# Spectral mixer with a token MLP: the channel transform back, even frequencies as two row-half products

## The chip, the cores and the metric

The kernel runs on one core of one Trainium2 chip. The metric is the device time of one launch in microseconds (us); the numbers below are medians over runs, and one further execution was taken by the hardware profiler.

## The reference

With x of 2048 tokens by 512 channels, everything in float32:

```
xn = layernorm(x, axis=-1)
s  = irfft2(rfft2(xn, axes=(tokens, channels)) * (w_r + 1j * w_i))       # global filter
h  = layernorm(xn, axis=-1)
u  = gelu(einsum("bsd,sf->bdf", h, w1) + b1)          # MLP over the tokens, F = 1792
g  = silu(einsum("bdf,fs->bds", u, w2) + b2) transposed back to tokens x channels
out = x + s * g
```

So there are two halves that meet in a product: a two-dimensional Fourier filter, and an MLP that mixes tokens.

## The kernel before, in words

Tokens lie in 16 tiles of 128. The Fourier transforms are written as matrix products with tables of cosines and sines that the host lays out (`_constants`): one along the channels, one along the tokens, and the same two backwards. The MLP's products are made from float32 numbers split in a high and a low part, three products for one (`hh`, `hl`, `w2f`); its second layer also uses a seven-product scheme in place of eight (`FORMS`, `ORDER`, `form_a` to `form_d`).

The work runs in three stages on TensorE. First the hidden layer of the MLP, with the forward transform over the tokens in its gaps. Then the rest of the hidden layer, with the filter. Last the stage that the change touches: a loop over `p` from 0 to 7, each block making two tiles of output tokens, `p` and `p + 8`.

A block `p` consists, on TensorE, of seven groups of products (`products(p, n)`, `n` in the order 1, 2, 5, 6, 3, 7, 4; each group 21 matmuls of a 128x128 stationary block of w2, tile `w2f`, against 256 moving columns). In one slot between two groups, which `SLOTS` fixes by hand (after the sixth group in most blocks, after the fourth in the last), stand the two small transforms of the spectral half: `spectral(p - 1)`, the token transform of the block before (tiles `y` and `cft`, 64x64 corners of the array), and `channels(p)`, the channel transform back (tiles `yt` and `cd`; the table `ci` is loaded over `cd`).

`channels(p)` before: for each of the two token tiles `i` and each of four groups `b` (real part of even k, real part of odd k, imaginary part of even k, of odd k; k is the channel frequency) one matmul of 128 frequencies by 128 tokens, stationary, against 128 columns of the table. Its result for `i` fills bank 6 + `i` of PSUM. By the mirror symmetry of the cosines the kernel needs only half the channel positions here; `unfolded(p)` makes the others by sums and differences.

`unfolded(p)` before: ScalarE copies the odd half from PSUM to `es`; VectorE adds and subtracts even and odd (two operations of 512 columns a partition, tile `es`); two more VectorE operations of 512 columns, real plus and minus imaginary part, write `y`, which `spectral(p)` reads in the next block's slot (in the last block, one group of products later). The letters of `SLOTS` say after which group each of the three pieces is put in the queues: an `s` is one piece of `unfolded`, a `g` one copy that makes the next `yt`.

Around them, in each block, ScalarE and VectorE split the next w2 tiles (`w2_high`, `w2_low`, tile `w2f`), add up w2 blocks (tile `a`), sum the products (tile `c`), apply the gate (`gate`, tile `g`) and multiply it with the spectral half (`finish`, tile `r`); GpSimd issues the loads of tile `s` and the stores to `out`. In this stage everything goes through `Kept`, which holds each engine to the order of the program, so an operation that is added to VectorE delays all that stand behind it in its queue.

A float32 matmul appears in the profile as two TensorE records (two passes), one of a product with `w2f` as one.

Of the kernel before, what the change touches and what calls it, by code (L numbers as in the profile page):

```python
# [12 lines left out]
AF = mybir.ActivationFunctionType  # L13
# [3 lines left out]
P = 128  # L17
# [27 lines left out]
def _k1(lo, hi):  # L45

    (t, h), s = divmod(hi, 2), 2 * lo + hi // 2
    return (64 - s if s else 32) if h else s


def _pairs(lo, t):


    if 2 * lo + t == 0:
        return np.array([[1, 0, 1, 0], [1, 0, -1, 0], [0, 1, 0, 0], [0, 0, 0, 1]], float)
    return np.array([[1, 0, 1, 0], [0, 1, 0, 1], [1, 0, -1, 0], [0, -1, 0, 1]], float)


def _constants():


    q = np.arange(P)
    a = 2 * np.pi * (np.outer(q, np.arange(32)) % P) / P
    f = np.stack([np.cos(a), np.sin(a)], 2)
    f[0::2, 0, 1], f[1::2, 0, 1] = np.cos(np.pi * q[0::2] / 2), np.sin(np.pi * q[1::2] / 2)
    f = np.concatenate([f[0::2], f[1::2]]).reshape(P, 64)

    a = 2 * np.pi * (np.outer(2 * np.arange(P) + 1, KD) % (2 * D)) / (2 * D)  # L70
    fd = np.stack([np.cos(a), -np.sin(a)])
    fd[1, :, 0] = np.cos(np.pi * np.arange(P))
    fd = fd.reshape(2, P, 2, P).transpose(0, 2, 1, 3).reshape(4, P, P)
    iv = fd.transpose(0, 2, 1) * 2.0 / (D * S)
    iv[0, 0] *= 0.5
    iv[2, 0] *= 0.5

    g = np.zeros((P, 8, 2, 32, 2))
    back = np.zeros((8, 2, P, 2, 64))
    freq = np.zeros((P, 8, 2), int)  # L80
    j = np.arange(16)
    for lo in range(16):
        for hi in range(4):
            k1, (n, l), (t, h) = _k1(lo, hi), divmod(lo, 2), divmod(hi, 2)
            for r in range(16):
                rows = cr, sr = np.arange(16) * 2 + hi * 32, np.arange(16) * 2 + hi * 32 + 1
                out = np.zeros((2, P))
                if k1:
                    k = [k1 + 128 * r] * 2
                    th = 2 * np.pi * ((j * k[0]) % S) / S  # L90
                    out[0, cr], out[0, sr] = np.cos(th), -np.sin(th)
                    out[1, cr], out[1, sr] = -np.sin(th), -np.cos(th)
                elif r == 0:
                    k = [0, S // 2]
                    out[0, cr], out[1, cr] = 1.0, np.cos(np.pi * j)
                else:
                    k = [128 * r if r < 8 else 64 + 128 * (r - 8)] * 2
                    th = 2 * np.pi * ((j * k[0]) % S) / S
                    out[0, rows[r >= 8]], out[1, rows[r >= 8]] = np.cos(th), -np.sin(th)
                rows = slice(64 * t, 64 * t + 64)  # L100

                out[:, rows] = np.einsum("sajb,abhc->shjc", out[:, rows].reshape(2, 2, 16, 2),
                                         _pairs(lo, t).reshape(2, 2, 2, 2)).reshape(2, 64)
                p = [l * 64 + 2 * (h * 16 + r) + c for c in range(2)]
                for s in range(2):
                    g[rows, n, l, h * 16 + r, s] = back[n, t, p[s], 0] = out[s, rows]
                    freq[p[s], n, t] = k[s]
                if k[0] == k[1]:
                    back[n, t, p[0], 1], back[n, t, p[1], 1] = -out[1, rows], out[0, rows]
                else:  # L110
                    back[n, t, p, 1] = out[:, rows]
    freq = freq.reshape(P, 16)


    ft = np.concatenate([np.concatenate([f[:64].T, f[64:].T], 1)] * 2)
    c = {
        "c_f": f.astype(np.float32),
        "c_ft": ft.astype(np.float32),
        "c_d": fd.transpose(1, 0, 2).astype(np.float32),
        "c_i": iv.transpose(1, 0, 2).astype(np.float32),  # L120
        "c_g": g.transpose(1, 0, 2, 3, 4).astype(np.float32),
        "c_h": back.transpose(0, 2, 1, 3, 4).astype(np.float32),
        "c_t": (np.array([-1.0, -2.0]) * np.where(q % 2, -1.0, 1.0)[:, None]).astype(np.float32),
    }
    return c, freq
# [13 lines left out]
def spectral_mixer_kernel(tc, x, w1, b1, w2, b2, wk, we, wx, c_f, c_ft, c_d, c_i, c_g, c_h, c_t, out):  # L139
    nc = tc.nc  # L140
    V, A, G, T, SY = nc.vector, nc.scalar, nc.gpsimd, nc.tensor, nc.sync
# [17 lines left out]
    with tc.tile_pool(name="ps", bufs=1, space=PSUM) as psp, ExitStack() as left, ExitStack() as right:  # L159
        ps = psp.tile([P, 8, 512], F32, name="ps")  # L160
# [8 lines left out]
        e1 = pers.tile([P, 16, 2], F32, name="e1")  # L169
# [78 lines left out]
        def new_h(j):  # L248
            return lnp.tile([P, D], F32, name=f"h{j}", tag="h", bufs=3)
# [186 lines left out]
        T = Kept(T, keep)  # L436
# [22 lines left out]
        h = new_h(0)  # L459
# [20 lines left out]
        for j in range(NJ):  # L480
# [11 lines left out]
            if j in (8, 10, 12, 14):  # L492
                q = slice(16 * (j - 8), 16 * (j - 6))
# [7 lines left out]
            if more:  # L501
                w = w1_tiles(j + 1)
                h = new_h(j + 1)
# [26 lines left out]
            if more:  # L530
                low(w[1][1], raws[j + 1, 1], w[1][0])
                if FIRST <= j < FIRST + NE:
                    i = j - FIRST
# [210 lines left out]
        for n in range(8):  # L744
            a, b, c, d, e, f = PACE[n]
            u, v, w = ([None] * (k < MADE[n]) for k in range(3))
# [89 lines left out]
        ci = cd  # L836
# [57 lines left out]
        V, A, SY, G = (Kept(e, keep) for e in (nc.vector, nc.scalar, nc.sync, nc.gpsimd))  # L894
# [3 lines left out]
        def new_sums(p):  # L898
            return (fp.tile([P, 2, 2, 2, P], F32, name=f"es{p}", tag="es"),
                    fp.tile([P, 2, 2, 2, P], F32, name=f"y{p}", tag="y"))  # L900
# [18 lines left out]

        def channels(p):  # L920

            yt = yts.pop(p)
            for i in range(2):
                pe = ps[:, 6 + i].rearrange("p (h b c) -> p h b c", b=2, c=P)
                for b in range(4):
                    T.matmul(pe[:, b % 2, b // 2], yt[:, i, b].rearrange("p e c -> p (e c)"), ci[:, b],
                             start=True, stop=True)

        def unfolded(p):

            pe = ps[:, 6:8].rearrange("p i (h k) -> p i h k", h=2)
            es, y = new_sums(p) if p else first_sums
            e0, e1 = (es[:, :, k].rearrange("p i b c -> p i (b c)") for k in range(2))
            A.activation(e1, pe[:, :, 1], AF.Copy)
            V.tensor_add(e0, pe[:, :, 0], e1)
            V.tensor_sub(e1, pe[:, :, 0], e1)
            yield
            u, v = es[:, :, :, 0], es[:, :, :, 1]
            V.tensor_add(y[:, :, :, 0], u, v)
            yield  # L940
            V.tensor_sub(y[:, :, ::-1, 1], u, v)
            ys[p] = y.rearrange("p i h q c -> p i (h q c)")
            yield

# [31 lines left out]
        for p in range(NP):  # L976
# [8 lines left out]
            for k, n in enumerate(ORDER):  # L985
# [23 lines left out]
                if k == slot:  # L1009
                    if p:  # L1010
                        spectral(p - 1)
                    channels(p)
                    pieces = unfolded(p)
                    if p:
                        for g, j in zip(gates.pop(p - 1), (j0 - 1, j1 - 1)):
                            finish(g, j, whole)
# [51 lines left out]
```

## Time and profile before

| | us |
|---|---|
| median of 3 runs (lowest, highest) | 377.51 (377.26, 377.56) |
| the profiled execution, its own time | 377.27 |
| its span, first to last instruction | 375.5 |
| TensorE busy in matmuls | 365.3 (97%) |
| VectorE busy | 300.2 (80%) |
| ScalarE busy | 211.9 (56%) |
| GpSimd busy | 86.7 (23%) |
| mean granted TensorE clock | 0.993 |

Times in rows of the profile are from the start of the span. PE is the matmul side of TensorE and PEld its weight loads, which overlap; DVE is VectorE, ACT is ScalarE. A row of the timeline gives start, length, engine, line, operation, destination and sources, shapes, how many instructions were merged, and in brackets how long the engine had been idle and what ended that. Line 136 is that of the helper class that records every operation, so groups are told apart by their tiles.

### The profile page before, as it was taken

How to read it: one execution, taken by the hardware profiler on the slowest of the kernel's cores; microseconds unless marked ns; L12 is line 12 of the kernel's file. 1: busy time of each engine (PE TensorE's matmuls, PEld its weight loads, DVE VectorE, ACT ScalarE, POOL GpSimd, SP SyncE). 2: the span in 40 equal slices, each digit the busy share in tenths (PEclk: the TensorE clock that was granted, in tenths of full speed). 3: DMA queues.
4: the chain of work that ended last, by engine and by line, in shares of the span. 5: the costliest groups of instructions: out<-in, count | busy, mean ns of one | idle time of the engine just before them, and what ended most of it. 6: DMA issues, size and time to landing. Idle time of an engine off the chain costs nothing.

```text
span 375.5 us, 8397 instructions
## 1 busy us (share of the span) xinstructions
PE 365.3 (97%) x3274; PEld 314.1 (84%) x3274; DVE 300.2 (80%) x564; ACT 211.9 (56%) x381; POOL 86.7 (23%) x128
## 2 busy tenths in 40 slices
PE   7999999999999999999999999999999999999991
PEld 4778888777887777877888999898989999898981
DVE  5799999965799987999985978676959685867771
ACT  4787888748534437545347675465464556464520
POOL 3133333331222202221020010230404040504031
PEclk9999999999999999999999999999999999999997
DMA  6967997407695596985493687798869787886343
GB/s 199 276 159 182 234 304 236 168 0 190 196 241 187 186 250 204 242 241 181 132 289 66 178 231 158 200 168 229 136 220 141 214 158 194 186 195 134 66 56 56
DMA packets 33288, 68.36 MB, mean 182 GB/s; under 512 B 4737, under 2 KB 19505, under 8 KB 33121
## 3 DMA queue, kind: packets, MB, share of 16 engines
q1 hardware_dynamic: 24192, 42.04, 39.5%
q0 software_dynamic: 8656, 25.27, 31.8%
q8 instruction: 25, 0.41, 0.5%
q10 hardware_dynamic: 400, 0.52, 0.5%
q14 instruction: 15, 0.11, 0.1%
HBM read 59.43 MB, written 8.13 MB: 180 GB/s over the span
## 4 chain that ended last, share of the span: by engine, by line
PE 96%; DVE 1%; DMA 1%; ACT 0%; issue 0%; DVEq 0%
PE ps L136 96%; DMA x<-in_x_dram 1%; DVE stm L216 0%; DVE rows L136 0%; ACT g L136 0%; DVE w1l L444 0%; DVE h L246 0%; ACT sdm L222 0%; DVE mvm L226 0%; DVE r0m L230 0%; DVE tm L232 0%; DVE rsm L233 0%; DVE tm L231 0%; DVE v2m L220 0%; DVE v2m L221 0%
## 5 line engine op out<-in xcount | busy, mean ns | idle before, releaser
L136 PE MATMUL ps<-h,w1h 128*128 128x512 f32 x400 | 116.5, 398 | 1.1 <-DVE nbm L235 1.1
L136 PEld LDWEIGHTS ps<-h,w1h 128*128 128x128 f32 x400 | 72.7, 188 | 20.9 <-issue 6.1
L136 PE MATMUL ps<-h,w1l 128*128 128x512 f32 x200 | 68.1, 392 | 0.1
L136 DVE TENSOR_TENSOR w2f<-a,w2f 128x896 fp32r<-128x896 f32 x36 | 39.3, 1092 | 27.8 <-ACT w2f L136 27.8
L136 PEld LDWEIGHTS ps<-h,w1l 128*128 128x128 f32 x200 | 37.2, 188 | 9.4 <-DVE w1l L444 1.6
L136 ACT ACTIVATE w2f<-a 128x896 fp32r<-128x896 f32 x36 | 36.6, 1018 | 13.5 <-issue 7.4
L136 PE MATMUL ps<-fb,w2f 128*128 128x256 f32 x336 | 42.9, 281 | 0.0
L136 PE MATMUL ps<-fa,w2f 128*128 128x256 f32 x336 | 42.3, 280 | 0.0
L136 PEld LDWEIGHTS ps<-fb,w2f 128*128 128x128 f32 x336 | 40.7, 188 | 0.9 <-issue 0.8
L136 POOL DMA_DIRECT2D s<-in_w_dram x14 | 18.2, 1300 | 99.4 <-DMA s<-in_w_dram 61.5
L136 PE MATMUL ps<-fc,w2f 128*128 128x256 f32 x336 | 40.9, 279 | 0.0
L136 PEld LDWEIGHTS ps<-fa,w2f 128*128 128x128 f32 x336 | 40.7, 188 | 0.0
L136 PEld LDWEIGHTS ps<-fc,w2f 128*128 128x128 f32 x336 | 40.1, 188 | 0.0
L136 POOL DMA_DIRECT2D out_dram<-r x28 | 23.7, 1288 | 31.7 <-DVE r L136 31.7
L152 ACT ACTIVATE w1h<-w1s 128x512 fp32r<-128x512 f32 x26 | 16.2, 631 | 20.9 <-PE ps L136 10.3
L626 POOL DMA_DIRECT2D xc<-xc x16 | 9.8, 617 | 70.4 <-ACT xc L624 55.1
L282 POOL TENSOR_TENSOR ey<-t 128x256 f32<-128x256 f32 x16 | 15.7, 981 | 43.5 <-DVE t L280 41.8
L136 DVE TENSOR_TENSOR w2f<-s,w2f 128x896 fp32r<-128x896 f32 x15 | 16.3, 1088 | 8.8 <-ACT w2f L136 8.8
L136 ACT ACTIVATE w2f<-s 128x896 fp32r<-128x896 f32 x15 | 15.4, 1024 | 12.4 <-PE ps L136 11.5
L444 DVE TENSOR_TENSOR w1l<-w1r,w1h 128x384 fp32r<-128x384 f32 x32 | 21.3, 667 | 0.5 <-ACT w1h L441 0.5
L136 PE MATMUL ps<-fd,w2f 128*128 128x256 f32 x168 | 21.1, 279 | 0.0
L136 ACT ACTIVATE g<-c,b2t 128x256 f32<-128x256 f32 x24 | 12.2, 507 | 14.8 <-DVE c L136 14.7
(115 smaller groups left out, 602.3 us busy)
## 6 DMA issues: line engine op xcount, KB each, us to landing
a<-in_w_dram SPq DMA_DIRECT2D x22, 448.0 KB, 3.7
wt<-in_wk_dram POOLq DMA_DIRECT2D x16, 512.0 KB, 5.9
s<-in_w_dram SPq DMA_DIRECT2D x16, 448.0 KB, 4.1
s<-in_w_dram POOLq DMA_DIRECT2D x16, 448.0 KB, 6.3
w1s<-in_w_dram SPq DMA_DIRECT2D x52, 128.0 KB, 5.5
w1r<-in_w_dram SPq DMA_DIRECT2D x28, 192.0 KB, 5.3
xc<-xc POOLq DMA_DIRECT2D x16, 256.0 KB, 3.0
out_dram<-in_x_dram SPq DMA_DIRECT2D x4, 960.0 KB, 7.2
```

The lines of the kernel that those rows point to most:

```text
L136: return lambda *args, **kw: self.keep(operation(*args, **kw))
L152: return A.activation(hi, src, AF.Copy), V.tensor_sub(lo, src, hi.bitcast(F32))
L282: G.tensor_add(ey[:, 0::3, :, j], a, b)
L444: keep(V.tensor_sub(dst, src, hi.bitcast(F32)))
L626: keep(G.dma_start(*(v.rearrange("p s t c -> p s (t c)") for v in (there[c::2], here[1 - c::2, ::-1]))))
```

## The change

For even k, the table's columns at the channel positions q and 127 - q differ only in the sign that k/2 decides: it is one for k divisible by 4 (rows 0 to 63 of `yt`) and the other for the rest (rows 64 to 127). So the change makes two products for each even group, one from each half of the rows, each with 64 columns instead of 128, and writes them to banks 6 and 7; their sum and their difference are the 128 columns that stood there before. The odd groups stay matmuls of 128 rows and 128 columns. In a block there are then 8 matmuls of 64 rows, 128 tokens, 64 columns, and 4 of 128 rows, 128 tokens, 128 columns, in place of 8 of the latter.

ScalarE copies one of the two even halves (256 columns, and one column more) instead of 512 odd columns, into `y`, which serves as room. VectorE makes the even columns with two operations of 256 columns, and then goes on as before, with the odd columns read from PSUM. The order in which the channel positions stand changes with it, and so the table (last lines of the first piece) and the ways in which `y` is written.

```diff
     iv = fd.transpose(0, 2, 1) * 2.0 / (D * S)
     iv[0, 0] *= 0.5
     iv[2, 0] *= 0.5
+    iv[1, :, 64:] *= -1
+    iv[1::2] = np.roll(iv[1::2], 64, 2)
...
         def channels(p):
             yt = yts.pop(p)
             for i in range(2):
-                pe = ps[:, 6 + i].rearrange("p (h b c) -> p h b c", b=2, c=P)
-                for b in range(4):
-                    T.matmul(pe[:, b % 2, b // 2], yt[:, i, b].rearrange("p e c -> p (e c)"), ci[:, b],
+                for s in range(2):
+                    for r, rows in enumerate((slice(0, 64), slice(64, P))):
+                        at = 128 * i + 64 * s
+                        T.matmul(ps[:, 6 + r, at:at + 64], yt[rows, i, 2 * s].rearrange("p e c -> p (e c)"), ci[rows, 2 * s, :64],
+                                 start=True, stop=True)
+            for i in range(2):
+                for s in (1, 0):
+                    at = 256 + 128 * s
+                    T.matmul(ps[:, 6 + i, at:at + P], yt[:, i, 2 * s + 1].rearrange("p e c -> p (e c)"), ci[:, 2 * s + 1],
                              start=True, stop=True)

         def unfolded(p):
-            pe = ps[:, 6:8].rearrange("p i (h k) -> p i h k", h=2)
             es, y = new_sums(p) if p else first_sums
+            other = y.rearrange("p i h q c -> p (i h q c)")[:, :257]
+            low_k, odd = ps[:, 6, :256].rearrange("p (i s c) -> p i s c", s=2, c=64), ps[:, 6:8, 256:]
+            A.activation(other, ps[:, 7, :257], AF.Copy)
+            other = other[:, :256].rearrange("p (i s c) -> p i s c", s=2, c=64)
+
+            V.tensor_add(es[:, :, 1, :, 64:], low_k, other)
+            V.tensor_sub(es[:, :, 1, :, 63::-1], low_k, other)
             e0, e1 = (es[:, :, k].rearrange("p i b c -> p i (b c)") for k in range(2))
-            A.activation(e1, pe[:, :, 1], AF.Copy)
-            V.tensor_add(e0, pe[:, :, 0], e1)
-            V.tensor_sub(e1, pe[:, :, 0], e1)
+            V.tensor_add(e0, e1, odd)
+            V.tensor_sub(e1, e1, odd)
             yield
             u, v = es[:, :, :, 0], es[:, :, :, 1]
-            V.tensor_add(y[:, :, :, 0], u, v)
+            to = y.rearrange("p i h q (n c) -> p i h (q n) c", n=2)[:, :, :, ::-3]
+            V.tensor_add(to, *(t.rearrange("p i h (n c) -> p i h n c", n=2) for t in (u, v)))
             yield
-            V.tensor_sub(y[:, :, ::-1, 1], u, v)
+            V.tensor_sub(y.rearrange("p i h q c -> p i h (q c)")[:, :, ::-1, 64:192], u, v)
```

TensorE, block 3: the slot between the sixth and the seventh group of products. Before (`128x64` and the like are the shapes of the result):

```order
L136 MATMUL ps_58<-fb6_2709,w2f7_3_3470 128x256
L136 MATMUL ps_58<-y2_3350,cft_63 64x512 x4
L136 MATMUL ps_58<-cd_64,yt3_3444 128x128 x8
L136 MATMUL ps_58<-fb2_1480,w2f4_3_3501 128x256
L136 MATMUL ps_58<-fb0_1592,w2f4_3_3501 128x256
```

The same place with the change:

```order
L138 MATMUL ps_58<-fb6_2709,w2f7_3_3488 128x256
L138 MATMUL ps_58<-y2_3366,cft_63 64x512 x4
L138 MATMUL ps_58<-cd_64,yt3_3462 128x64 x8
L138 MATMUL ps_58<-cd_64,yt3_3462 128x128 x4
L138 MATMUL ps_58<-fb2_1480,w2f4_3_3519 128x256
```

Eight whole products became eight of half the rows and half the columns and four whole ones; what stands ahead and behind is the same.

VectorE, from the end of block 2 into block 3: `r` is the gated product of the block before, `es` and `y` are `unfolded`, `a` the sums of w2 blocks, `w2f` the low parts that the coming products read. Before:

```order
L136 TENSOR_TENSOR r_3344<-ps,g_2918 128x2x128 x2
L136 TENSOR_TENSOR es_3349<-ps,es_3349 128x2x256 x2
L136 TENSOR_TENSOR a_3_3179<-a_3_3179,s_11_3146 128x896
L136 TENSOR_TENSOR a_3_3206<-a_3_3206,a_3_3179 128x896
L136 TENSOR_TENSOR w2f_3_3377<-s_11_3146,w2f_3_3377 128x896
L136 TENSOR_TENSOR y_3350<-es_3349 128x4x128
L136 TENSOR_TENSOR w2f_3_3410<-a_3_3179,w2f_3_3410 128x896
L136 TENSOR_TENSOR y_3350<-es_3349 128x2x2x128
L136 TENSOR_TENSOR w2f_3_3437<-a_3_3206,w2f_3_3437 128x896
```

With the change:

```order
L138 TENSOR_TENSOR r_3360<-ps,g_2924 128x2x128 x2
L138 TENSOR_TENSOR es_3365<-ps,y_3366 128x2x2x64 x2
L138 TENSOR_TENSOR es_3365<-es_3365,ps 128x2x256 x2
L138 TENSOR_TENSOR a_3_3191<-a_3_3191,s_11_3158 128x896
L138 TENSOR_TENSOR a_3_3218<-a_3_3218,a_3_3191 128x896
L138 TENSOR_TENSOR w2f_3_3395<-s_11_3158,w2f_3_3395 128x896
L138 TENSOR_TENSOR y_3366<-es_3365 128x4x2x64
L138 TENSOR_TENSOR w2f_3_3428<-a_3_3191,w2f_3_3428 128x896
L138 TENSOR_TENSOR y_3366<-es_3365 128x2x2x128
L138 TENSOR_TENSOR w2f_3_3455<-a_3_3218,w2f_3_3455 128x896
```

Two operations of 256 columns a partition are new, ahead of the two sums of w2 blocks and the low parts; the rest stands in the same order.

## The prediction

> **What bounds the kernel now.** I read the page first: the span, the engines and the chain of work that ended last.
>
> ```profile
> span 375.5 us, 8397 instructions
> PE 365.3 (97%) x3274; PEld 314.1 (84%) x3274; DVE 300.2 (80%) x564; ACT 211.9 (56%) x381; POOL 86.7 (23%) x128
> ...
> PE 96%; DVE 1%; DMA 1%; ACT 0%; issue 0%; DVEq 0%
> ```
>
> TensorE is the chain: 96% of it lies there. Whatever the change takes from TensorE or gives to it in the last stage moves the end, and VectorE counts only where it makes TensorE wait. The view by stretches, over one block of the last stage, shows how much room VectorE has:
>
> ```profile
> core 0: us, PE busy (x) PEld busy (x) DVE busy (x) ACT busy (x) POOL busy (x), PEclk, DMA share, GB/s
> 262.00:282.35 20.35, 20.35 (x174) 19.41 (x173) 15.00 (x23) 10.80 (x17) 5.17 (x6) 1.00 0.76 176
> ```
>
> A block lasts 20.35 us, TensorE is busy for all of it at the full granted clock (1.00), VectorE for 15.00. So 5.35 us a block are free on VectorE, if they lie in the right places. Next I read TensorE's weight loads around one slot, since it is there that eight matmuls change form:
>
> ```profile
> 279.11 0.31 PEld L136 LDWEIGHTS ps<-fb,w2f 128*128 128x128 f32 x2
> 279.55 0.21 PEld L136 LDWEIGHTS ps<-y,cft 64*64 64x64 f32 x8
> 280.57 1.86 PEld L136 LDWEIGHTS ps<-cd,yt 128*128 128x128 f32 x16 [0.81 <-issue]
> 282.35 0.30 PEld L136 LDWEIGHTS ps<-fb,w2f 128*128 128x128 f32 x2
> ```
>
> The eight matmuls of the channel transform are 16 records, and from their first load to the next group's first load is 282.35 - 280.57 = 1.78 us: 0.111 us a record. Half of them are the even groups: 8 x 0.111 = 0.89 us a block, 7.1 us in all eight blocks. That is everything the change has to work with on TensorE.
>
> **What a record costs: the moving columns or the load.** The change halves the moving columns of the even groups, so it matters whether the 0.111 us are set by those columns or by the load of 128x128 weights. The warm-up at the kernel's start has a case that tells these apart, matmuls of single-pass type with 128 moving columns; the products with `w2f` are of the same type with 256:
>
> ```profile
> 5.41 0.72 PE L136 MATMUL ps<-wz 128*128 128x128 f32 x5
> ...
> L136 PE MATMUL ps<-wz 128*128 128x128 f32 x6 | 0.8, 266 | 0.0
> ...
> 262.04 2.54 PEld L136 LDWEIGHTS ps<-fb,w2f 128*128 128x128 f32 x21
> 264.51 2.54 PEld L136 LDWEIGHTS ps<-fd,w2f 128*128 128x128 f32 x21
> ```
>
> 21 products of 256 columns take 264.51 - 262.04 = 2.47 us, 0.118 each. The warm-up's five of 128 columns take 0.72 us with one record's 0.27 at the end, so (0.72 - 0.27) / 4 = 0.112 each. Half the moving columns saved 0.006, not 0.059. At 128 columns of one pass the load sets the pace: 0.112 us for a stationary block of 128x128. The new even records have 64 columns in two passes, as much moving work as those warm-up records, so they too should go at the pace of their loads. What is left is the load of 64 rows by 128 columns, which this trace does not have. The nearest rows are the 64x64 tiles of the forward transform:
>
> ```profile
> L136 PEld LDWEIGHTS ps<-cf,h 64*64 64x64 f32 x512 | 8.3, 134 | 3.2 <-ACT h L242 0.7 <-ACT cf L254 0.7 <-ACT w1h L441 0.7
> ...
> 51.94 1.02 PEld L136 LDWEIGHTS ps<-cf,h 64*64 64x64 f32 x64 [0.35 <-ACT w1h L441]
> 53.03 0.19 PEld L136 LDWEIGHTS ps<-h,w1h 128*128 128x128 f32 x1
> ```
>
> 64 loads on four corners are 16 rounds, and (1.02 - 0.13) / 15 = 0.059 us a round. So tiles that share no rows do load side by side, and a load of half the rows and half the columns takes about half of 0.112. Whether that is for the rows or for the columns the trace can't say. I take the columns: four corners fill the whole array in 0.059 where one whole load takes 0.112, so filling is not limited by the number of cells, while each row has to take twice as many weights one after the other in a block of 128 columns. Then one round of the new pairs, two loads of 64 rows side by side, takes 0.112 as a whole load did, and 16 records in 8 rounds take the same 0.89 us as the 8 whole ones. The even half gains nothing.
>
> The Trainium skill ("TensorE: Matmul & The Clock Gate", section "LDWEIGHTS (loading the stationary operand)") says the same of the load: its time goes by the columns, and few rows take as long as 128. By that rule the even half stays at 0.89 us; no run here shows the shape yet.
>
> **What the change adds on TensorE: two ways of tiling the array where there was one.** Going between 64x64 and 128x128 costs something in the rows above. From the second `fb` load (279.11 + 0.12 = 279.23) to the first of `y` is 0.32 us instead of 0.118: 0.20 more. On the way back, the last round of `cf` begins at 51.94 + 15 x 0.059 = 52.83 and the next whole load at 53.03: 0.20 instead of 0.059, 0.14 more. So the array empties before it goes on in another form, for 0.14 to 0.20 us. Before, a slot has two such changes, `fb` to `y` and `y` to `yt`, and none between `yt` and `fb`. After, the order is `fb`, `y` (64x64), even pairs (64x128), odd groups (128x128): one more in each of the 8 slots, and in block 0, which has no `y`, also one on the way in. I take 0.15 for the way out, nearest to the row with short moving operands, and 0.20 for the way in: 8 x 0.15 + 0.20 = 1.4 us slower. With 0.14 everywhere it is 1.3; with 0.20 everywhere 1.8. If a first matmul after each change waits for its load on top of that, the upper bound rises: the longest of the whole records is 377 ns against 275.
>
> ```profile
> L136 PE MATMUL ps<-cd,yt x128: 270/275/377, 219.6 to 358.7; 128*128 128x128 f32 x128
> ```
>
> That is 0.10 more for nine changes, 1.8 + 0.9 = 2.7 us.
>
> **What it adds on VectorE, and what hides it.** The rows of `es` and `y`, and those of 256 columns:
>
> ```profile
> L136 DVE TENSOR_TENSOR es<-ps,es x16: 678/687/692, 223.5 to 360.3; 128x512 f32<-128x512 f32 x16
> L136 DVE TENSOR_TENSOR y<-es x16: 682/684/687, 228.0 to 362.4; 128x512 f32<-128x512 f32 x16
> ...
> L136 ACT ACTIVATE es<-ps x8: 579/601/602, 222.8 to 359.0; 128x512 f32<-128x512 f32 x8
> ...
> L136 ACT ACTIVATE p<-ps 128x256 f32<-128x256 f32 x12 | 4.6, 385 | 10.5 <-PE ps L136 10.5
> ...
> L136 DVE TENSOR_TENSOR r<-ps,g 128x256 f32<-128x256 f32 x24 | 8.5, 415 | 0.0
> ```
>
> Four operations of 0.68 remain; two of 256 columns come to them, 0.42 each alone. ScalarE's copy falls from 0.60 to about 0.39. So VectorE has 2 x 0.42 = 0.84 us more a block, or 0.66 where operations overlap (four of `r` take 1.41 in the rows below: 0.33 each). Behind them stand the two sums into `a` and the low parts in `w2f`, which TensorE needs. This is the queue after the slot of block 2:
>
> ```profile
> 261.89 1.41 DVE L136 TENSOR_TENSOR r<-ps,g 128x256 f32<-128x256 f32 x4
> 263.21 1.41 DVE L136 TENSOR_TENSOR es<-ps,es 128x512 f32<-128x512 f32 x2
> ...
> 266.66 1.08 DVE L136 TENSOR_TENSOR w2f<-s,w2f 128x896 fp32r<-128x896 f32 x1
> 267.67 0.68 DVE L136 TENSOR_TENSOR y<-es 128x512 f32<-128x512 f32 x1
> 268.63 1.09 DVE L136 TENSOR_TENSOR w2f<-a,w2f 128x896 fp32r<-128x896 f32 x1 [0.28 <-ACT w2f L136]
> 269.64 0.69 DVE L136 TENSOR_TENSOR y<-es 128x512 f32<-128x512 f32 x1
> 270.87 1.09 DVE L136 TENSOR_TENSOR w2f<-a,w2f 128x896 fp32r<-128x896 f32 x1 [0.55 <-ACT w2f L136]
> ...
> 269.57 5.11 PE L136 MATMUL ps<-fc,w2f 128*128 128x256 f32 x42
> ```
>
> The tightest is the `w2f` that ends at 267.74: TensorE starts on that block at 269.57 and reads the low part for the last 7 of its 21 matmuls, from 269.57 + 14 x 0.118 = 271.2. Even 0.84 us late it is there 2.6 us ahead. The gaps of 0.28 and 0.55 then take up the 0.84, and VectorE is on its old times after 270.9. In the last block the result is wanted sooner, one group of products after the slot:
>
> ```profile
> 358.31 1.41 DVE L136 TENSOR_TENSOR r<-ps,g 128x256 f32<-128x256 f32 x4
> 359.63 1.41 DVE L136 TENSOR_TENSOR es<-ps,es 128x512 f32<-128x512 f32 x2
> 361.44 0.42 DVE L136 TENSOR_TENSOR c<-ps,v 128x256 f32<-128x256 f32 x1 [0.41 <-PE ps L136]
> 361.79 1.28 DVE L136 TENSOR_TENSOR y<-es 128x512 f32<-128x512 f32 x2
> ...
> 363.81 1.09 PE L136 MATMUL ps<-y,cft 64*64 64x512 f32 x8
> ```
>
> `y` is ready at 363.07, TensorE takes it at 363.81 when its own turn comes: 0.74 to spare. The wait of 0.41 swallows part of the 0.84, so `y` comes at most 0.43 late, and 0.3 is left. I cost VectorE and ScalarE at nothing; without this cover the last block would cost up to 0.4 us and a whole block's lateness would cost 0.84.
>
> **The sum.** +1.4 us on TensorE, nothing elsewhere. The profiled execution took 377.27 in all with its span of 375.5; its median of three runs is 377.51, 0.24 above. I add to the median: 377.51 + 1.4 = 378.9 us (a span of about 376.9).
>
> **The rivals.** What a measurement of this kernel can tell from no change is about 0.2%, 0.75 us.
>
> *The half-height load takes half the time* (faster). If a load goes by the cells it fills, a round of pairs takes 0.059 like the corners' rounds and the even half of a block falls by 8 x (0.111 - 0.059) = 0.42 us, 3.3 in eight blocks; less the 1.4 that is -1.9, so 375.6. It decides from a round of about 0.09: there the saving, 64 x 0.02, meets the 1.4. For it speaks that the corners' time fits both readings; against it, what each row has to take in. The Trainium skill ("TensorEngine Tiling (Array Packing)", section "Theoretical Speedup") grants up to twice the speed for a dimension of 64 or less, which is this outcome; the rows here show such side by side work only for corners that are small both ways. 0.13.
>
> *No emptying between `y` and the pairs* (the same). Both use halves of the rows; if the array passes from one to the other without the 0.15 to 0.20 that such a change costs, seven slots get 1.05 to 1.4 back and the sum is 0 to +0.35: 377.5 to 377.9, middle 377.7. For it speaks that the row halves are the same in both; against it, that the columns are not. "TensorEngine Tiling (Array Packing)", section "Key Properties", in the Trainium skill, has any change of the mode empty TensorE, so by it this doesn't happen; the rows above agree for the changes they show. 0.13.
>
> *The halves take turns* (the pairs don't run as pairs). Then 16 loads of 0.111 stand where 8 did: +7.1, with the 1.4 it is +8.5, 386.0. Against it speak the corners, where row halves do load side by side. 0.05.
>
> *VectorE reaches the chain*: the new operations write reversed and split columns, and if they took twice as long, 0.84 more a block, the last block's `y` would be 0.5 us late and the tightest `w2f` still in time: +1.9, 379.4. 0.05.
>
> The forecast itself: 0.64. So faster 0.13; the same 0.13; slower 0.64 + 0.05 + 0.05 = 0.74. The range leaves out the faster case and the turns, 0.18: from 377.3, just under the second rival's 377.5 by the spread of the runs, to 377.51 + 2.7 = 380.2.
>
> **What would show it.** In the profile after, the loads of the 64-row matmuls should come in pairs every 0.112 us, 0.9 us for 16, and between the last of them and the first whole load should be about 0.20 - 0.06 + 0.11 = 0.25 us. The slot of blocks 1 to 7, from the first `yt` load to the next `w2f` load, should be 1.9 to 2.0 us instead of 1.78. VectorE's four `es` operations should take about 2.1 us, with no wait of TensorE for VectorE in a block. Loads in pairs every 0.06 us, or a slot under 1.6 us, would make me wrong on the load; a slot at 1.78 wrong on the emptying.

## The result, and the profile after

The changed kernel took 378.88 us (median of 21 runs, 378.39 to 379.70), the kernel before 377.22 (21 runs, 373.29 to 378.41). The ratio is 1.0081, with a 95% interval of 1.0055 to 1.0108: slower by 3.05 us, where 1.4 was forecast. That is the difference of the means, 378.88 against 375.83; the medians are only 1.66 apart, because the median of before happens to fall among its longer times. The time itself, 378.9, is the forecast one; what differs is the kernel before. Its 21 times lie at two levels: ten from 373.29 to 374.32 (mean 373.8) and eleven from 377.22 to 378.41 (mean 377.7). The three runs and the profile that the prediction started from were all of the upper level. The 21 times of the changed kernel lie at one level.

The profile of before was taken at the upper level too. Against it, the profile after differs by what the prediction added. First the page, then TensorE's weight loads around the slot of block 3:

```profile
span 376.9 us, 8549 instructions
PE 366.8 (97%) x3338; PEld 314.9 (84%) x3338; DVE 305.6 (81%) x580; ACT 210.3 (56%) x381; POOL 86.7 (23%) x128
```

```profile
280.27 0.21 PEld L138 LDWEIGHTS ps<-y,cft 64*64 64x64 f32 x8
281.29 2.01 PEld L138 LDWEIGHTS ps<-cd,yt 64*128 64x128 f32 x24 [0.81 <-issue]
283.22 0.30 PEld L138 LDWEIGHTS ps<-fb,w2f 128*128 128x128 f32 x2
```

The span is 376.9, as forecast: 1.4 longer. The slot from the first `yt` load to the next `w2f` load is 283.22 - 281.29 = 1.93 us, against 1.78. From the first load of `y` to the first of `yt` it is 1.02 us, as it was before (280.57 - 279.55). VectorE's queue after the slot of block 2, and its part in the last block with TensorE's next use of `y`:

```profile
262.47 1.41 DVE L138 TENSOR_TENSOR r<-ps,g 128x256 f32<-128x256 f32 x4
263.80 0.75 DVE L138 TENSOR_TENSOR es<-ps,y 128x256 f32<-128x256 f32 x2
264.65 1.41 DVE L138 TENSOR_TENSOR es<-es,ps 128x512 f32<-128x512 f32 x2
265.98 1.08 DVE L138 TENSOR_TENSOR a<-a,s 128x896 f32<-128x896 f32 x1
...
268.10 1.08 DVE L138 TENSOR_TENSOR w2f<-s,w2f 128x896 fp32r<-128x896 f32 x1
...
271.62 1.09 DVE L138 TENSOR_TENSOR w2f<-a,w2f 128x896 fp32r<-128x896 f32 x1 [0.23 <-ACT w2f L138]
...
363.46 1.28 DVE L138 TENSOR_TENSOR y<-es 128x512 f32<-128x512 f32 x2
```

```profile
365.26 1.09 PE L138 MATMUL ps<-y,cft 64*64 64x512 f32 x8
```

From the first `es` to the sum `a` it is 265.98 - 263.80 = 2.18 us instead of 264.54 - 263.21 = 1.33 (the sum `a` of before began at 264.54): 0.85 more. By 271.62 VectorE waits for ScalarE again, so the lateness is taken up, and in the last block `y` is ready at 364.74, 0.52 ahead of TensorE. Nothing here explains the other 1.65 us of the measured 3.05.

### The profile page after: what moved, and what is told of

Same layout as the page of the kernel before. It is cut to its first block, busy times and chain, and to the rows that moved or that the text cites. A ratio compares the mean times of both kernels' runs of the same rounds, so it can differ in the third digit from the quotient of the medians.

```text
span 376.9 us, 8549 instructions
## 1 busy us (share of the span) xinstructions
PE 366.8 (97%) x3338; PEld 314.9 (84%) x3338; DVE 305.6 (81%) x580; ACT 210.3 (56%) x381; POOL 86.7 (23%) x128
## 4 chain that ended last, share of the span: by engine, by line
PE 96%; DVE 1%; DMA 1%; ACT 0%; issue 0%; DVEq 0%
PE ps L138 96%; DMA x<-in_x_dram 1%; DVE stm L218 0%; DVE rows L138 0%; ACT g L138 0%; DVE w1l L446 0%; DVE h L248 0%; ACT sdm L224 0%; DVE mvm L228 0%; DVE r0m L232 0%; DVE tm L233 0%; DVE rsm L235 0%; DVE tm L234 0%; DVE v2m L222 0%; DVE v2m L223 0%
## 5 line engine op out<-in xcount | busy, mean ns | idle before, releaser
L138 PEld LDWEIGHTS ps<-cd,yt 64*128 64x128 f32 (+1 forms) x192 | 15.5, 188 | 6.4 <-issue 4.9
```

The costliest lines, as they stand in the source:

```text
L138: return lambda *args, **kw: self.keep(operation(*args, **kw))
```

## The experiments

**The kernel before, once more; VectorE's part alone; TensorE's part alone; half the columns.** The four ran on one chip and share the runs of the kernel before.

`e1_before` has no edit.

> The kernel before, unchanged. Its 21 times lie at two levels, ten at 373.3 to 374.3 us and eleven at 377.2 to 378.4 us, while the changed kernel's 21 all lie at 378.4 to 379.7. If the two levels belong to the kernel or to the chip and not to the change, this copy shows both levels again, about 3.9 us apart, and its profile falls on one of them: the row-by-row difference to the profile of before then says what the lower level does faster. If the lower level was an accident of that chip, all times lie within 0.5 us of 377.5.

Measured: seven of 12 times from 373.37 to 374.50, five from 377.50 to 378.04, and of the 29 runs of before beside it 22 from 373.37 to 374.80 and seven from 377.23 to 377.88. Both levels are there, and the profile (span 371.6) fell on the lower. The loads of the same products in it, after the slot of block 2:

```profile
259.60 1.86 PEld L136 LDWEIGHTS ps<-cd,yt 128*128 128x128 f32 x16 [0.81 <-issue]
261.38 2.46 PEld L136 LDWEIGHTS ps<-fb,w2f 128*128 128x128 f32 x21
263.77 2.45 PEld L136 LDWEIGHTS ps<-fd,w2f 128*128 128x128 f32 x21
266.15 2.45 PEld L136 LDWEIGHTS ps<-fa,w2f 128*128 128x128 f32 x21
```

The slot is as before (261.38 - 259.60 = 1.78). But 21 products of `fd` take 266.15 - 263.77 = 2.38 us, 0.113 each, where the prediction's rows had 2.47, 0.118. In this execution all products of the last stage up to the slot of block 1 run at 118 ns and all from there on at 113. Those are 43 groups of 21, each 0.09 us shorter: 3.9 us, the distance of the levels. From here on, 113 ns is called the fast rhythm and 118 the slow one.

Neither the clock nor more memory traffic goes with the slow rhythm. Here is one stretch by engines, first in the profile of before, then in this one:

```profile
core 0: us, PE busy (x) PEld busy (x) DVE busy (x) ACT busy (x) POOL busy (x), PEclk, DMA share, GB/s
262.10:278.00 15.90, 15.90 (x137) 15.90 (x137) 11.94 (x18) 8.73 (x14) 4.31 (x5) 1.00 0.76 160
...
262.10:278.00 15.90, 15.90 (x143) 15.90 (x142) 12.31 (x17) 8.59 (x14) 4.32 (x5) 1.00 0.83 177
```

The granted clock is 1.00 in both, and the faster execution moved more by DMA (177 GB/s against 160), not less.

`e2_vector_part`:

```diff
             A.activation(e1, pe[:, :, 1], AF.Copy)
+            V.tensor_add(room_, ps[:, 6, :256], had)
+            V.tensor_sub(room_[:, ::-1], ps[:, 6, :256], had)
             V.tensor_add(e0, pe[:, :, 0], e1)
```

> The kernel before with VectorE's part alone: two more operations of 256 columns ahead of the sums and differences of each block, into room that is overwritten later. TensorE is as before. My theory: hidden, the profiled span stays within 0.2 us of 375.5 and the slot of block 3 (first yt load to the next w2f load) at 1.78 us. Rival, that VectorE reaches the chain: 0.3 to 0.8 us more a block or in the last block, a span of 375.9 to 381. If the extra two operations are what keeps a kernel off the lower level, all times lie near 377.5 and none near 373.7.

Measured: ratio 0.9998 (0.9966 to 1.0029); ten of 12 times from 373.91 to 374.44, two at 377.39 and 377.86. The two operations cost nothing and don't keep the kernel off the lower level. My figure for the span was written for the upper level; the profile fell on the lower, with a span of 372.3 and the slot at 1.78 us as expected. In it the fast rhythm began at the slot of block 2, one block later than in `e1_before`, so the place of the turn is not fixed.

`e3_tensor_part`: `channels` of the change with `unfolded` of before.

> TensorE's part alone: the 64-row pairs and four whole matmuls of the change, but ScalarE and VectorE with the operations of before (a copy of 512 columns, four operations of 512). Left out: the sum and the difference of the halves, and the changed table. My theory: span 375.5 + 1.4 = 376.9, slot 1.92 us, pairs every 0.112 us. If TensorE's part keeps the kernel off the lower level, all times lie near 378.9; if VectorE's part does, some lie near 373.7 + 1.4 = 375.1.

Measured: 378.97 us, six times from 378.86 to 379.22, ratio 1.0109 (1.0067 to 1.0151). No time at the lower level, the products at 118 ns in all blocks. The whole of the result is in TensorE's part. The span, 377.4, is 0.5 over my figure, the time is not; the 0.5 lies ahead of the last stage, where the first `yt` load comes at 220.41 instead of the changed kernel's 219.91.

`e4_half_columns`:

```diff
                 for b in range(4):
-                    T.matmul(pe[:, b % 2, b // 2], yt[:, i, b].rearrange("p e c -> p (e c)"), ci[:, b],
+                    n = P if b % 2 else 64
+                    T.matmul(pe[:, b % 2, b // 2, :n], yt[:, i, b].rearrange("p e c -> p (e c)"), ci[:, b, :n],
```

> The kernel before with 64 instead of 128 moving columns in the even groups, with whole loads of 128x128 and no other form of tiling. Left out: half of the even columns. If the load sets the pace (my theory) the slot stays at 1.78 us and the span at 375.5 although a quarter of the moving work is gone; if the moving columns do, the slot falls by 8 x 0.055 = 0.44 us to 1.34 and the span by 3.5 us to 372.0.

```profile
279.34 1.86 PEld L136 LDWEIGHTS ps<-cd,yt 128*128 128x128 f32 x16 [0.81 <-issue]
281.12 0.19 PEld L136 LDWEIGHTS ps<-fb,w2f 128*128 128x128 f32 x1
```

Measured: slot 281.12 - 279.34 = 1.78 us, no change, though half of the even groups' moving columns are gone; ratio 1.0000 (0.9963 to 1.0036), nine of 12 times at the lower level (373.46 to 374.94). The load sets the pace.

**What in TensorE's part keeps the products at 118 ns.** `e5_corners` cuts the even pairs once more; `e6_more_whole` issues the odd groups twice; `e7_odd_only` is the kernel before without its even groups; `e8_odd_first` has the odd groups ahead of the pairs.

```diff
-                        T.matmul(ps[:, 6 + r, at:at + 64], yt[rows, i, 2 * s].rearrange("p e c -> p (e c)"), ci[rows, 2 * s, :64],
+                        for e in range(2):
+                            T.matmul(ps[64 * e:64 * e + 64, 6 + r, at:at + 64], yt[rows, i, 2 * s, e], ci[rows, 2 * s, :64],
                                  start=True, stop=True)
```

> The changed kernel with the even pairs cut once more, by tokens, into 64x64 corners: 16 matmuls of 64 rows, 64 tokens, 64 columns, in the same form of tiling as y ahead of them. The result is the same. My theory of the load: a round of four corners takes 0.059 us, the even half falls from 0.89 to 0.47 us a block, and the extra change of form is gone in blocks 1 to 7, so -0.42 x 7 - 0.1 = -3.0 us against before at the same rhythm of the products: a span of 372.5 if the products run at 118 ns, 368.6 if most run at 113 ns. On the two rhythms: if the 64x128 form keeps the products at 118 ns, this one shows 113 ns in some executions, as the kernel before does; if eight whole matmuls ahead of the products (instead of 16) keep them there, it never does and all its times lie within 1 us of each other near 374.3.

```profile
278.86 0.21 PEld L138 LDWEIGHTS ps<-y,cft 64*64 64x64 f32 x8
279.34 0.15 PEld L138 LDWEIGHTS ps<-cd,yt 64*64 64x64 f32 x4 [0.28 <-issue]
...
281.23 0.19 PEld L138 LDWEIGHTS ps<-fb,w2f 128*128 128x128 f32 x1
```

```profile
242.11 2.46 PEld L138 LDWEIGHTS ps<-fb,w2f 128*128 128x128 f32 x21
...
256.39 2.46 PEld L138 LDWEIGHTS ps<-fb,w2f 128*128 128x128 f32 x21
...
261.35 2.54 PEld L138 LDWEIGHTS ps<-fb,w2f 128*128 128x128 f32 x21
...
276.18 2.54 PEld L138 LDWEIGHTS ps<-fb,w2f 128*128 128x128 f32 x21
...
281.23 2.46 PEld L138 LDWEIGHTS ps<-fb,w2f 128*128 128x128 f32 x21
```

Measured: 373.14 us, 11 times from 372.74 to 373.68, ratio 0.9917 (0.9886 to 0.9949): faster than the kernel before by the means, though its times overlap with before's lower level (373.42 to 374.68 beside it), and faster than the changed kernel. From the first `y` load to the next product is 281.23 - 278.86 = 2.37 us, 0.43 less than before's 2.80. What I had expected of the rhythm was wrong either way: it is neither kept nor absent, but in this profile changes at every slot from block 1 on (2.46 us for 21 loads is 113 ns, 2.54 is 118).

> The changed kernel with its four odd matmuls issued twice, so that 16 whole records instead of 8 stand between the 64x128 pairs and the products, as many as in the kernel before. At 118 ns a product: 378.9 + 8 x 8 x 0.112 = 386.0 us. If the number of whole records decides the rhythm, some executions fall to the lower level, about 3.9 us below; if the 64x128 form does, none.

Measured: 386.16 us, six times from 385.88 to 386.94; 118 ns throughout. Sixteen whole records don't bring 113 ns back.

> The kernel before with the even groups left out: 8 whole records instead of 16 stand between the 64x64 matmuls and the products, and no other form of tiling. At 118 ns a product: 377.5 - 8 x 0.89 = 370.4 us. If the number of whole records decides the rhythm, all times lie there; if the 64x128 form does, some lie 3.9 us lower, near 366.5.

Measured: three times from 366.87 to 367.59 and three from 370.97 to 371.61. Both levels, with eight whole records. So their number is not what decides.

> The changed kernel with the odd groups ahead of the even pairs, so that the products follow the 64x128 form directly. One more change of form in blocks 1 to 7 than in the changed kernel (64x64 to whole to 64x128 to whole): if a change costs 0.14 to 0.20 us, the span is 1.0 to 1.4 us longer, 377.9 to 378.3, at 118 ns a product. If the change of form costs nothing and the pairs' own pace made the difference, it stays at 376.9. If no whole record ahead of the products lets them start at 113 ns, the lower level shows, near 374.3.

```profile
280.46 0.21 PEld L138 LDWEIGHTS ps<-y,cft 64*64 64x64 f32 x8
281.48 2.06 PEld L138 LDWEIGHTS ps<-cd,yt 128*128 128x128 f32 x24 [0.81 <-issue]
283.60 0.19 PEld L138 LDWEIGHTS ps<-fb,w2f 128*128 128x128 f32 x1
```

Measured: 380.54 us (379.83 to 380.81), all blocks at 118 ns. From the first `y` load to the product is 3.14 us, 0.19 over the changed kernel's 2.95: one more change of form, at the upper end of its price.

**Where the 113 ns are lost.** `e9_half_pairs` has before's matmuls for `p < 4` and the pairs for the rest.

> TensorE as before in blocks 0 to 3 and with the change's pairs in blocks 4 to 7; ScalarE and VectorE as before. Left out: the sum and the difference of the halves, and the changed table. All blocks at 118 ns: 377.5 + 4 x 0.145 = 378.1 us. If a slot with the pairs puts the products back to 118 ns, executions that come to 113 ns in blocks 1 to 3 lose it in block 4 and their times lie between 375.9 and 377.5, none lower. If a slot with the pairs only never lets them in, those executions keep 113 ns and lie near 374.5.

```profile
295.92 2.45 PEld L136 LDWEIGHTS ps<-fb,w2f 128*128 128x128 f32 x21
298.50 0.21 PEld L136 LDWEIGHTS ps<-y,cft 64*64 64x64 f32 x8
299.52 2.01 PEld L136 LDWEIGHTS ps<-cd,yt 64*128 64x128 f32 x24 [0.81 <-issue]
301.45 2.54 PEld L136 LDWEIGHTS ps<-fb,w2f 128*128 128x128 f32 x21
303.92 2.54 PEld L136 LDWEIGHTS ps<-fd,w2f 128*128 128x128 f32 x21
```

Measured: 376.58 us, 11 of 12 times from 375.95 to 377.24 and one at 378.27; the runs of before beside it lie at 373.05 to 374.43 (24) and 377.21 to 377.65 (five). The rows show the moment: the last products ahead of the first slot with pairs run at 113 ns, those behind it at 118, and stay there to the end. Here the pairs do not merely fail to let the fast rhythm in; the slot with them ends it.

`e10_corners_first` puts the corners ahead of `y`; `e11_flip_once` does so from block 2 on; `e12_pairs_first` puts the pairs ahead of `y`:

```diff
                 if k == slot:
+                    evens(p)
                     if p:
                         spectral(p - 1)
-                    channels(p)
+                    odds(p)
```

> The 64x64 corners once more, with the even corners ahead of y instead of behind it, so that the whole odd matmuls follow y directly, as the whole matmuls do in the kernel before. The result is the same. At 118 ns in all blocks 377.5 - 3.0 = 374.5 us. If what decides the rhythm is what stands between y and the products, the two levels of before come back, and the lower is 3.0 us under its 374, near 371. If it is the form of the even half wherever it stands, the products change their rhythm in every block as with the corners behind y, and all times lie near 373.

Measured: 371.92 us, seven of 12 times from 370.77 to 372.02 and five from 374.54 to 375.49; ratio 0.9962 (0.9923 to 1.0000). Two levels (means 371.5 and 375.1), each about 2.3 us below its like of the runs of before beside it (373.8 and 377.4), where 3.0 was expected. The profile fell on the upper, at 118 ns throughout.

> The corners behind y in block 1, where they turned 118 ns into 113 in the profile of the corners, and ahead of y in blocks 2 to 7, where I expect the rhythm to be kept. If the rhythm is set by the slot in this way, all times lie at the lower level, 370.7 to 371.5 us, with none at 374. If the rhythm is chance at each return, times spread from 371 to 374.5.

Measured: three times from 370.92 to 371.61 and nine from 374.50 to 375.56. The profile (375.18 us) stayed at 118 ns behind the slot of block 1, so that slot doesn't turn the rhythm reliably; this expectation fell.

> The changed kernel with one reordering: its 64x128 pairs stand ahead of y instead of behind it, so that the whole odd matmuls and the products follow the 64x64 form of y, as in the kernel before. The result is the same, and so is the number of changes of form. If what stands between y and the products keeps them at 118 ns, both levels come back: 378.9 us at 118 ns and about 375 at 113. If the pairs anywhere in the slot do it, all times stay at 378.4 to 379.7.

Measured: 378.92 us, ten times from 378.52 to 379.40. No lower level: with the pairs at either place the kernel stays at the upper. But not every such slot comes out slow: in its profile the products behind the last slot run at 113 ns (2.46 us). Its rows, first the pairs by themselves in block 3, then that last slot:

```profile
280.31 0.97 PEld L138 LDWEIGHTS ps<-cd,yt 64*128 64x128 f32 x16
281.35 0.21 PEld L138 LDWEIGHTS ps<-y,cft 64*64 64x64 f32 x8
...
357.20 1.06 PEld L138 LDWEIGHTS ps<-cd,yt 64*128 64x128 f32 x16
358.33 0.21 PEld L138 LDWEIGHTS ps<-y,cft 64*64 64x64 f32 x8
359.35 0.97 PEld L138 LDWEIGHTS ps<-cd,yt 128*128 128x128 f32 x8 [0.81 <-issue]
360.24 2.46 PEld L138 LDWEIGHTS ps<-fa,w2f 128*128 128x128 f32 x21
```

Eight rounds of two loads in 0.97 us, (0.97 - 0.19) / 7 = 0.111 a round. In the last slot they took 1.06, so the break was 0.09 us longer there; whether that let the fast rhythm in is not shown.

**The form, or the number of changes.** `e13_corner_between` adds four 64x64 matmuls between before's even and odd groups; `e14_apart` moves the changed kernel's `y` one group ahead, `e15_y_apart` the kernel before's:

```diff
-                if k == slot:
-                    if p:
-                        spectral(p - 1)
+                if k == slot - 1 and p:
+                    spectral(p - 1)
+                if k == slot:
                     channels(p)
```

> The kernel before with one round of 64x64 corner matmuls (four, 64 columns) between its even and its odd whole groups, into columns of PSUM that the odd groups overwrite. The result is the same. That is two more changes of form in every slot and no 64x128 form: 377.5 + 8 x (0.06 + 0.20 + 0.15) = 380.8 us at 118 ns. If the number of changes of form in a slot keeps the products at 118 ns, all times lie there; if the 64x128 form does, both levels show, the lower near 376.9.

Measured: 381.35 us, six times from 381.02 to 381.87; 118 ns in all blocks. So it is not the 64x128 form alone.

> The changed kernel with y taken out of the slot, one group of products earlier: the slot then has two changes of form (products to 64x128 to whole), as many as the kernel before, and y's place two of its own. The result is the same. One more change in blocks 1 to 7: 378.9 + 7 x 0.15 to 0.20 = 380.0 to 380.3 us at 118 ns. If the number of changes in a slot keeps the products at 118 ns, both levels show, the lower near 376; if the 64x128 form does, all times lie near 380.

```profile
258.21 2.45 PEld L138 LDWEIGHTS ps<-fb,w2f 128*128 128x128 f32 x21 [0.81 <-issue]
260.79 2.01 PEld L138 LDWEIGHTS ps<-cd,yt 64*128 64x128 f32 x24
262.71 2.54 PEld L138 LDWEIGHTS ps<-fb,w2f 128*128 128x128 f32 x21
```

Measured: 380.68 us, six times from 380.11 to 380.94. No lower level, with two changes of form in the slot; so it is not three changes in the slot alone either. But the rhythm did turn: in blocks 2, 4 and 6 the one group between `y` and the slot ran at 113 ns, and each time the slot with the pairs put the products back to 118, as the rows show for block 2.

> The kernel before with y taken out of the slot, one group of products earlier. The result is the same. The block still has two changes of form (products to y and back), but the products follow the 64x64 form directly, and the whole matmuls of the channel transform follow products without a change. At 118 ns 377.5 us, as before. If the number of changes of form in a block decides (two let the products at 113 ns, three or four don't), both levels show, the lower near 374. If the products must come from whole float32 matmuls that follow a change of form, as in every kernel so far that reached 113 ns, all times lie near 377.5.

```profile
257.45 0.21 PEld L136 LDWEIGHTS ps<-y,cft 64*64 64x64 f32 x8
258.47 2.46 PEld L136 LDWEIGHTS ps<-fb,w2f 128*128 128x128 f32 x21 [0.81 <-issue]
260.85 1.87 PEld L136 LDWEIGHTS ps<-cd,yt 128*128 128x128 f32 x16
```

Measured: 377.77 us, 12 times from 376.95 to 378.01: no lower level with two changes of form a block. But one group in its profile, directly behind `y` in block 2, ran at 113 ns (2.46 us in the rows), and the groups after the whole matmuls were at 118 again, without any pairs in the slot. Both of my explanations are refuted: the count of changes is not enough, and the fast rhythm can begin without whole float32 matmuls ahead of it.

## Why the prediction was right or wrong

*The load sets the pace*: right, and shown twice. With half the moving columns in the even groups the slot stayed at 1.78 us, and the pairs run at 0.111 us a round, not 0.06. That refutes the faster rival. The trace agrees with the Trainium skill ("TensorE: Matmul & The Clock Gate", section "LDWEIGHTS (loading the stationary operand)"), by which the time of a load goes by its columns and not by its rows. Here a round of two loads of 64 rows by 128 and one load of 128 by 128 both take 0.11 us. The corners, with half the stationary columns, gained 0.43 us a slot, against 0.42 worked out.

*The extra change of form*: right. The slot grew by 1.93 - 1.78 = 0.15 us, the span by 1.4, and a further change in the kernel with the odd groups first cost 0.19. From the start of the last round of pairs (281.29 + 7 x 0.111 = 282.07) to the first whole load, at 282.33, it is 0.26 us; 0.25 was worked out. The rival without emptying is refuted: from the first load of `y` to the first of the pairs it is 1.02 us, as long as to whole matmuls, while corners behind `y` follow after 0.48 (279.34 - 278.86 in `e5_corners`). The halves don't take turns.

*VectorE hidden*: right. Its two operations took 0.85 us instead of 0.66 to 0.84, and alone they changed nothing (0.9998).

*The sum*: wrong. It priced what the change does in the slot and took all other products as they stood, at 0.118 us, "nothing elsewhere"; and it set that against 377.51, the upper of two levels. The failed step is the reading of 0.118 as a price of the product itself. It is one of two rhythms, and the kernel before reaches the other, 0.113, in part of its executions: ten of 21. From upper level to the changed kernel it is 378.88 - 377.7 = 1.2 us, the forecast within its spread; the other part of the 3.05, 10 / 21 x 3.9 = 1.9 us, is the fast rhythm that the change takes away.

That the time itself came out at the forecast 378.9 is therefore in part luck: the changed kernel keeps the slow rhythm that the prediction took for granted. And the 3.05 belongs to this set of runs: the share of before's times at the lower level went from 7 of 16 (beside `e5_corners`) to 24 of 29 (beside `e9_half_pairs`), and with 24 of 29 the same change would come out at 1.2 + 24 / 29 x 3.9 = 4.4 us, as an estimate. For the same reason 0.2% was too fine a limit for telling a change from none; with 21 runs of each kernel the interval is still 0.27% to either side.

That TensorE's part takes the fast rhythm away is shown (no time at the lower level in 21 and 6 runs, against ten of 12 with VectorE's part alone), and that a slot with the pairs puts fast products back to slow is seen once in the half-and-half kernel and three times in `e14_apart`. The three runs and the one profile that the prediction had could not have told it: they were all at the slow rhythm. What could be seen was that the floor of the load, 0.112, lay below the 0.118 of the products and that nothing explained the 0.006 between them; I used the difference and didn't ask for its cause.

What stays open is why. In all these profiles the rhythm of the last stage changed only where the stream of products was broken, and then held until the next break. The slot of before (`y`, then whole matmuls; also in `e2_vector_part`, `e4_half_columns`, `e7_odd_only` and the first half of `e9_half_pairs`) turned it from 118 to 113 ns at block 1 or 2 in four of six profiles and never back; by its two levels, the kernel with the corners ahead of `y` does the like. The pairs behind `y` and a corner round between whole groups left or put it at 118. With the corners behind `y` it alternated in the one profile. The rest is mixed: pairs ahead of `y` let 113 in at the last slot only; behind `y` in a place of its own the products ran at 113 in three of seven blocks (`e14_apart`) and in one of seven (`e15_y_apart`), and the slot that followed put them back each time, with pairs or without. No single property of the slot that I tried sorts all these kernels, and no run varied the length of a break in small steps.

## What to carry to other kernels

Halving the moving columns of a matmul that already runs at the pace of its weight load gained nothing here (1.78 us a slot with all columns and with half of the even ones); cut the stationary block's columns as well, so that the load shrinks with it, and keep the pieces in a form of tiling that stands beside them anyway (here 64x64 corners next to other 64x64 corners: 0.43 us a block gained where row halves lost 0.15). Before a change of less than 1% is priced against a time, look at enough runs of the kernel to see whether its times have more than one level, and take a profile of each: a rhythm of all products can be worth more than the edit.

## What the hardware showed that I had not expected

A stream of identical load-and-multiply pairs (128x128 weights, 256 columns) ran steadily at either 113 or 118 ns at the same granted clock of 1.00, for whole blocks of 147 products, in the same kernel with the same work on all other engines. Which of the two it was changed only at breaks of the stream. In the last stage that is worth 3.9 us of 377, more than the 1.4 us that the change added in its own slots.
